# First batch's keys and values in one product, V loaded ahead of the queries, and another pattern of products of nothing

## The chip, the cores and the metric

The kernel runs on one core of one Trainium2 chip. The metric is the time of one execution on the device in microseconds. A core has TensorE for matrix products (in the profile PE, its weight loads PEld), VectorE (DVE), ScalarE (ACT) and GpSimd (POOL) for the rest, and SyncE (SP), which here issues nearly all DMAs. All engines run on their own, each in the order of its own list of instructions, and wait for each other by semaphores.

## The reference

Attention over 32 memory slots per head, then a mixture of experts. There are 8 batches, 8 heads, 576 tokens, head size 64; the experts have inner size 1024 and outer size 512.

```
a = softmax of phi over the 576 tokens
k_m = einsum('bhsm,bhsd->bhmd', a, k)
v_m = einsum('bhsm,bhsd->bhmd', a, v)
attn = softmax(q @ k_m^T / 8)
x = attn @ v_m, heads side by side: 4608 x 512
logits = x @ w_gate + modality_bias[modality_id]
e = argmax(logits); gate = its softmax probability
out = gate * (relu(x @ w1[e]) @ w2[e])
```

All arrays are float32.

## The kernel before

The kernel goes through the eight batches one after the other. For each batch it makes a memory of keys and values (`mem_max`, `mem_top`, `mem_exp`, `mem_sums`, then `kv_products` and `kv_divide`), turns them (`keys_turn`, `values_turn`), forms scores with the queries (`scores`, L420 in the profile), softens and normalises them on VectorE and ScalarE (`soften`, `normalise`) and splits the result into an upper and a lower part (`a_split`, tiles xah and xal, for the second half of the tokens xbh and xbl). The values are multiplied into the first expert weights (`value_products`, L561, tiles vwh and vwl), so that `hidden` (L594) gets from the attention weights straight to the inner layer, and `outputs` (L623) does the second expert product. Every one of these products is done as three terms of upper and lower parts. One expert is guessed at the start (`guess`), its weights are loaded, and a second pass for other experts runs only if the guess is wrong for some token; with these inputs it does not run.

The order of the work is written by a planner. There are two lists of stages, `attention` and `experts`; each stage has a kind (`TAKES` gives what it is thought to take on TensorE and what chain of other engines follows), the stages it comes after, a due place in the progress of the experts, and a `floor`, a planner's time before which it is not put in. `weave` merges the two lists by these numbers, and what it calls in turn is what each engine's list gets. The floors stand for the landing of loads. `plan_first` writes the stages of batch 0 up to its second scores, by hand.

At the start TensorE has nothing to do until the first loads land. `warm(n)` issues n products of a zero tile called `busy` into a PSUM bank that nobody reads (L152); `warm(BUSY)` does 38 of them at once, and `nothing(n)` stages stand between the stages of `plan_first`.

For batch 0 keys and values are separate in the kernel before. `kv_products(0, range(1))` multiplies the softened phi with the keys (L310 into the tile pair, 72 products), then with the column of ones for the sums (L319, 8 products). The values come in two pieces: five of nine chunks behind the keys, the other four behind the first scores (L310 into the tiles pe). `kv_divide` divides the keys (L340) and later the values (L338). From batch 1 on one call does both, with 128 columns instead of 64. A float32 product stands in the trace as two products and two weight loads, so that the 72 products of the keys are x144 there.

`load_kv`, `load_queries` and `load_phi` issue loads on SyncE's queue. For batch 0 the order is phi, K, the queries' first four chunks, V, the other five chunks; then come the token types, the gate's weights, and behind `guess` the two halves of the first expert weights (raw1), the second ones (raw2, in four loads), and batch 1's phi, K, V and queries (`more_keys`). The second expert weights are split in `first_w2` (casts on ScalarE L653, rests on GpSimd L654).

PSUM has two pairs of banks, pair0 and pair1 (`pair_of_banks`), and four single banks `pe`. The name "pa" is the first bank of pair0, "mem" the first of pair1.

## Time and profile before

| what | us |
|---|---|
| median of 3 runs (lowest, highest) | 410.91 (410.58, 411.28) |
| the profiled execution | 410.64 |
| its span in the trace | 408.9 |
| TensorE busy | 390.9 |
| VectorE busy | 238.7 |
| ScalarE busy | 143.7 |
| first product of L594 | 32.07 from the span's start |
| first product of L623 | 39.95 |

Times in the trace are from the span's start. A row of the timeline has the start, the time from the first to the last of merged instructions, engine, line, operation, what it writes and reads, shapes and count, and in brackets how long the engine was idle before and what ended that. "issue" there is time in which the engine waited for nothing that the profile shows. A busy TensorE is not TensorE at its peak, since products overlap in the pipeline. From 34 us to the end TensorE has hardly a gap.

### The profile page before, as it was taken

How to read it: one execution, taken by the hardware profiler on the slowest of the kernel's cores; microseconds unless marked ns; L12 is line 12 of the kernel's file. 1: busy time of each engine (PE TensorE's matmuls, PEld its weight loads, DVE VectorE, ACT ScalarE, POOL GpSimd, SP SyncE). 2: the span in 40 equal slices, each digit the busy share in tenths (PEclk: the TensorE clock that was granted, in tenths of full speed). 3: DMA queues.
4: the chain of work that ended last, by engine and by line, in shares of the span. 5: the costliest groups of instructions: out<-in, count | busy, mean ns of one | idle time of the engine just before them, and what ended most of it. 6: DMA issues, size and time to landing. Idle time of an engine off the chain costs nothing.

```text
span 408.9 us, 10298 instructions
## 1 busy us (share of the span) xinstructions
PE 390.9 (96%) x4350; PEld 312.4 (76%) x4350; DVE 238.7 (58%) x581; ACT 143.7 (35%) x342; POOL 39.6 (10%) x79
## 2 busy tenths in 40 slices
PE   8679998999999999999999999999999999989994
PEld 6437796688858879688867879687877879778983
DVE  3555773976688566773487447774388537861400
ACT  1218143433333325343442425242343424341410
POOL 3326302001100200002000200002000110000000
PEclk9758999999999999999999999999999999999998
DMA  7999046824471292526711274432602011341112
GB/s 233 358 387 340 30 111 209 304 101 139 144 282 31 81 332 69 211 73 207 252 27 27 83 264 140 151 133 63 222 2 51 27 29 28 129 157 26 28 27 58
DMA packets 28968, 56.92 MB, mean 139 GB/s; under 512 B 3312, under 2 KB 8432, under 8 KB 28912
## 3 DMA queue, kind: packets, MB, share of 16 engines
q1 hardware_dynamic: 28624, 56.16, 41.4%
q8 instruction: 36, 0.59, 0.6%
q14 instruction: 20, 0.16, 0.1%
q10 hardware_dynamic: 288, 0.01, 0.0%
HBM read 37.29 MB, written 18.87 MB: 137 GB/s over the span
## 4 chain that ended last, share of the span: by engine, by line
PE 87%; DVE 3%; ACT 3%; issue 3%; DMA 2%; POOL 1%; SPq 0%; ACTq 0%; POOLq 0%
PE pe L623 49%; PE pe L594 23%; PE pe L561 4%; PE pair L420 3%; PE pair L310 3%; DMA q_sb<-in_q_dram 2%; PE pair L508 1%; PE pair L140 1%; DVE hl L606 1%; ACT exp L283 1%; ACT hh L603 1%; ACT ob L636 1%; PE pair L561 0%; PE pair L152 0%; PE pair L274 0%
## 5 line engine op out<-in xcount | busy, mean ns | idle before, releaser
L623 PE MATMUL pe<-w2h,hh 128*128 128x512 f32 x288 | 117.9, 409 | 0.4 <-DVE hl L606 0.4
L623 PE MATMUL pe<-w2h,hl 128*128 128x512 f32 x288 | 112.5, 390 | 0.0
L623 PE MATMUL pe<-w2l,hh 128*128 128x512 f32 x288 | 110.4, 391 | 0.0
L606 DVE SCALAR_TENSOR_TENSOR hl<-pe,hh 128x256 fp32r<-128x256 f32 (+2 forms) x160 | 58.6, 393 | 53.8 <-ACT hh L603 53.2
L623 PEld LDWEIGHTS pe<-w2h,hh 128*128 128x128 f32 x288 | 54.0, 188 | 25.3 <-issue 12.9
L603 ACT ACTIVATE hh<-pe 128x256 fp32r<-128x256 f32 (+2 forms) x160 | 53.7, 362 | 38.9 <-PE pe L594 38.5
L623 PEld LDWEIGHTS pe<-w2l,hh 128*128 128x128 f32 x288 | 54.0, 188 | 12.0
L623 PEld LDWEIGHTS pe<-w2h,hl 128*128 128x128 f32 x288 | 54.2, 188 | 9.4
L636 ACT ACTIVATE ob<-pe,gates 128x512 f32<-128x512 f32 x36 | 24.7, 689 | 82.6 <-PE pe L623 41.9
L594 PE MATMUL pe<-xbh,vwh 128*128 128x320 f32 x128 | 39.8, 311 | 0.0
L594 PE MATMUL pe<-xbl,vwh 128*128 128x320 f32 x128 | 39.6, 309 | 0.0
L594 PE MATMUL pe<-xbh,vwl 128*128 128x320 f32 x128 | 39.5, 309 | 0.0
L594 PE MATMUL pe<-xah,vwh 128*128 128x256 f32 x128 | 37.1, 292 | 0.2 <-DVE hl L606 0.2
L594 PE MATMUL pe<-xal,vwh 128*128 128x256 f32 x128 | 36.2, 285 | 0.1
L594 PE MATMUL pe<-xah,vwl 128*128 128x256 f32 x128 | 35.3, 283 | 0.0
L249 POOL TENSOR_TENSOR t2sums<-exp 128x512 f32<-128x512 f32 x7 | 9.0, 1286 | 262.2 <-ACT exp L283 262.2
L594 PEld LDWEIGHTS pe<-xah,vwh 128*128 128x128 f32 x128 | 24.7, 193 | 3.0 <-ACT xah L488 1.7
L447 DVE STREAM_TRANSPOSE a<-pair 128x256 f32<-128x256 f32 (+1 forms) x32 | 13.6, 461 | 21.3 <-PE pair L420 21.3
L594 PEld LDWEIGHTS pe<-xal,vwh 128*128 128x128 f32 x128 | 24.6, 192 | 0.6 <-DVE xal L491 0.3
L594 PEld LDWEIGHTS pe<-xbh,vwh 128*128 128x128 f32 x128 | 24.1, 188 | 0.5 <-issue 0.2
L594 PEld LDWEIGHTS pe<-xbl,vwh 128*128 128x128 f32 x128 | 24.1, 188 | 0.3
L594 PEld LDWEIGHTS pe<-xah,vwl 128*128 128x128 f32 x128 | 24.0, 191 | 0.3 <-issue 0.3
(117 smaller groups left out, 444.1 us busy)
## 6 DMA issues: line engine op xcount, KB each, us to landing
kv_sb<-in_k_dram SPq DMA_DIRECT2D x8, 1152.0 KB, 6.4
kv_sb<-in_v_dram SPq DMA_DIRECT2D x8, 1152.0 KB, 8.8
out_dram<-ob SPq DMA_DIRECT2D x64, 128.0 KB, 2.4
q_sb<-in_q_dram SPq DMA_DIRECT2D x7, 1152.0 KB, 6.4
ph<-in_phi_dram SPq DMA_DIRECT2D x8, 576.0 KB, 4.3
raw<-in_moe_w_dram SPq DMA_DIRECT2D x2, 1024.0 KB, 9.5
raw<-in_moe_w_dram SPq DMA_DIRECT2D x1, 1280.0 KB, 12.4
out_dram<-ob SPq DMA_DIRECT2D x4, 256.0 KB, 2.1
```

Of the source, the lines that this page charges most:

```text
L140: nc.tensor.transpose(dst, src, ident[:rows, :rows])
L249: eng.tensor_tensor(t2, src[:, :, 0:4 * M], src[:, :, 4 * M:8 * M], op=op)
L283: nc.scalar.activation(px[:, :, cs], px[:, :, cs], AF.Exp)
L310: nc.tensor.matmul(kvp[g][M * j:M * (j + 1)], lhsT=pe[half, j, c * M:(c + 1) * M], rhs=kv_sb[half, ts.start:ts.stop, j, c * D:(c + 1) * D] ...
L420: nc.tensor.matmul(sc[g][M * j:M * (j + 1), a, c0 * BL:(c0 + n) * BL].rearrange("p (c t) -> p c t", t=BL), lhsT=kTs[b % 2][p0:p0 + BL, u, ...
L447: nc.vector.transpose(a[:, g].rearrange("p a c m -> p a (c m)"), sc[g][:, :, RA * part * BL:(RA * part + n) * BL])
L561: nc.tensor.matmul(pvs[g][M * j:M * (j + 1), :], lhsT=vT[b][rows, j, :], rhs=raw1[rows, j, cols], start=True, stop=True, tile_position=(D ...
L594: nc.tensor.matmul(ph[:, 0:n], lhsT=(vl if k == 2 else vh)[:, g, cols], rhs=xl if k == 1 else xh, start=(g == k == 0), stop=(g == NG - 1 a ...
L603: nc.scalar.activation(hs[0][:, f, h0:h0 + p1 - p0], ph[:, p0:p1], AF.Relu)
L606: nc.vector.scalar_tensor_tensor(hl, ph[:, p0:p1], 0.0, hh.bitcast(F32), op0=ALU.max, op1=ALU.subtract)
L623: nc.tensor.matmul(po, lhsT=tile_columns(hl if n == 1 else hh, f, t), rhs=(w2l if n == 2 else w2h)[:, f, :], start=(f == n == 0), stop=(f ...
L636: nc.scalar.activation(ob, po, AF.Copy, scale=gate_of(b, t))
```

## The change

The keys and values of batch 0 are multiplied together, as in the other batches, in one call of `kv_products(b)` into one pair of banks; `kv_divide(b)` divides both. V is loaded ahead of the queries. The first 38 products of nothing become 92 small ones (32 x 64 instead of 128 x 256) and two large ones (128 x 512, twice as wide as before). Between the stages of `plan_first` the products of nothing are all of the large kind, and there are fewer of them ahead of the keys (2 and 6 instead of 4 and 22) and some more behind. The turned keys and values of batch 0 go to pair0 instead of pair1, and some planner's floors are later.

```
-    BUSY = 38
+    BUSY = 92, 2
...
-    busy = const.tile([P, 256], BF16, name="busy")
+    busy = const.tile([P, 512], BF16, name="busy")
...
-    def warm(n):
+    def warm(n, small=False, name="pa"):
         if n > 0:
-            idle = bank("pa")
+            idle = bank(name)
             for _ in range(n):
-                nc.tensor.matmul(idle[:, 0:256], lhsT=busy[:, 0:P], rhs=busy, start=True, stop=True)
+                if small:
+                    nc.tensor.matmul(idle[0:BL, 0:64], lhsT=busy[:, 0:BL], rhs=busy[:, 0:64], start=True, stop=True)
+                else:
+                    nc.tensor.matmul(idle, lhsT=busy[:, 0:P], rhs=busy, start=True, stop=True)
...
-    def kv_products(b, ts, banks=None, cs=range(QC)):
+    def kv_products(b):
...
+        pk = pair_of_banks(1)
+        live["psum"] = pk[:, :, 2 * D]
+        live["kvp"] = pk[:, :, 0:2 * D].rearrange("p g (t d) -> p g t d", t=2)
+        for c in range(QC):
...
-                        kvp[g][M * j:M * (j + 1)], lhsT=pe[half, j, c * M:(c + 1) * M],
-                        rhs=kv_sb[half, ts.start:ts.stop, j, c * D:(c + 1) * D],
+                        live["kvp"][M * j:M * (j + 1), g], lhsT=pe[half, j, c * M:(c + 1) * M],
+                        rhs=kv_sb[half, :, j, c * D:(c + 1) * D],
...
-        live["pkv"] = pair_of_banks(1)
+        live["pkv"] = pair_of_banks(1 if b else 0)
...
-            live["pkv"] = pair_of_banks(1)
+            live["pkv"] = pair_of_banks(0)
...
+        nothing(2)
+        add(("exp", 0), "first exp", [("top", 0)], mem_exp, 0)
+        nothing(6)
+        add(("prepare",), "nothing", [], prepare)
+        add(("sums", 0), "first sums", [("exp", 0)], mem_sums, 0)
+        add(("kv", 0), "kv0", [("exp", 0)], kv_products, 0, floor=11.7)
+        turns(0, 0, 13.1)
+        add(("kn", 0), "kvn", [("kv", 0)], kv_divide, 0)
+        turns(0, 1, 13.1)
+        add(("more", 0), "nothing", [], more_keys, 0)
         nothing(4)
-        add(("exp", 0), "first exp", [("top", 0)], mem_exp, 0)
-        nothing(22)
-        add(("prepare",), "nothing", [], prepare)
-        turns(0, 0, 9.6)
-        add(("sums", 0), "first sums", [("exp", 0)], mem_sums, 0)
-        turns(0, 1, 9.6)
-        add(("k", 0), "k", [("exp", 0)], kv_products, 0, range(1), floor=8.5)
-        add(("kn", 0), "kn", [("k", 0), ("sums", 0)], kv_divide, 0, range(1))
-        v = range(1, 2)
-        add(("v", 0, 0), "v1", [], kv_products, 0, v, two_banks, range(RB), floor=12.8)
+        add(("kT", 0), "kT", [("kn", 0)], first_keys)
+        nothing(2)
         for k in range(2):
-            turns(1, k, 14.3)
-        add(("kT", 0), "kT", [("kn", 0)], first_keys)
-        nothing(6)
+            turns(1, k, 14.8)
         add(("s", 0, 0), "s0", [("kT", 0), ("qt", 0, 0, 1)], scores, 0, 0, RA)
         add(("e", 0, 0, 0), "e", [("s", 0, 0)], soften, 0, 0, None, 0)
-        add(("v", 0), "v2", [], kv_products, 0, v, None, range(RB, QC))
-        add(("vn", 0), "vn", [("v", 0)], kv_divide, 0, v)
+        nothing(3)
+        add(("kvT", 0), "vT", [("s", 0, 0)], first_values)
         add(("e", 0, 0, 1), "e", [], soften, 0, 0, None, 1)
         nothing(3)
-        add(("kvT", 0), "vT", [("vn", 0)], first_values)
-        add(("more", 0), "nothing", [], more_keys, 0)
         add(("n", 0, 0, 2), "n", [("e", 0, 0, 1)], normalise, 0, 0)
-        nothing(3)
-        add(("vw", 0, 0), "vwp", [("kvT", 0)], value_products, 0, 0, pair_(0), floor=17.0)
+        add(("vw", 0, 0), "vwp", [("kvT", 0)], value_products, 0, 0, pair_(0), floor=18.2)
         add(("vwu", 0, 0), "vwu", [("vw", 0, 0)], value_upper, 0)
-        add(("vw", 0, 1), "vwp", [], value_products, 0, 1, pair_(1), floor=19.7)
+        nothing(4, "pe")
+        add(("vw", 0, 1), "vwp", [], value_products, 0, 1, pair_(1), floor=21.0)
+        nothing(6, "pe")
...
-            stage(experts, ("w2", c), "w2", [], first_w2, c, floor=23.4 if c < W2N else 25.6)
+            stage(experts, ("w2", c), "w2", [], first_w2, c, floor=24.3 if c < W2N else 26.4)
...
-    plan_steps(0, evenly(1.9, 0.25))
+    plan_steps(0, evenly(1.4, 0.25))
...
-        load_kv(0, 0)
+        for t in range(2):
+            load_kv(0, t)
         load_queries(0, 0, RA)
-        load_kv(0, 1)
         load_queries(0, RA, RB)
...
-        warm(BUSY)
+        warm(BUSY[0], True)
+        warm(BUSY[1])
```

On TensorE the first place is the end of the opening products of nothing and the turn of phi's maxima (tile top) behind them. Before:

```order
L152 LDWEIGHTS busy
L152 MATMUL pair_154<-busy 128x256
L140 MATMUL pair_217<-ident,top 128x128 [waits DVE_49,Pool_49]
L152 LDWEIGHTS busy
L152 MATMUL pair_243<-busy 128x256 [waits PE_49]
```

and now:

```order
L154 LDWEIGHTS busy
L154 MATMUL pair_154<-busy 32x64
L156 LDWEIGHTS busy
L156 MATMUL pair_247<-busy 128x512 [waits PE_49]
L156 LDWEIGHTS busy
L156 MATMUL pair_247<-busy 128x512
L141 MATMUL pair_274<-ident,top 128x128 [waits DVE_49,Pool_49]
```

The turn of top (old L140, new L141) stood behind 76 instructions of nothing and now stands behind 188.

The second place on TensorE is the products of softened phi (tile exp) with keys and values (kv_sb), and the sums behind them. Before, the values (into pe) follow the keys' sums at once:

```order
L310 MATMUL pair_318<-kv_sb,exp 32x64 [waits DVE_49,DMAHW3_49,PE_49,Activation_49]
L310 MATMUL pair_318<-kv_sb,exp 32x64 x39
L310 MATMUL pair_318<-kv_sb,exp 32x64 [waits Activation_49]
L310 MATMUL pair_318<-kv_sb,exp 32x64 x31
L319 MATMUL pair_318<-ones_c,sums 32x1 [waits DVE_49,Pool_49]
L319 MATMUL pair_318<-ones_c,sums 32x1 x7
L310 MATMUL pe<-kv_sb,exp 32x64 [waits DMAHW5_49]
L310 MATMUL pe<-kv_sb,exp 32x64 x39
```

and now:

```order
L307 MATMUL pair_355<-kv_sb,exp 32x128 [waits DMAHW3_49,DVE_49,DMAHW4_49,PE_49,Activation_49]
L307 MATMUL pair_355<-kv_sb,exp 32x128 x39
L307 MATMUL pair_355<-kv_sb,exp 32x128 [waits Activation_49]
L307 MATMUL pair_355<-kv_sb,exp 32x128 x31
L315 MATMUL pair_355<-ones_c,sums 32x1 [waits DVE_49,Pool_49]
L315 MATMUL pair_355<-ones_c,sums 32x1 x7
L156 LDWEIGHTS busy
L156 MATMUL pair_451<-busy 128x512 [waits PE_49]
```

The first product now waits for two loads, K and V, where it waited for K alone; products of nothing stand where the values stood, and the values' 72 products of their own are gone.

SyncE's first loads stood in this order (ph is phi, q_sb the queries):

```order
L159 DMA ph_102<-in_phi_dram 128x4x288
L162 DMA kv_sb<-in_k_dram 128x4x576
L166 DMA q_sb_99<-in_q_dram 128x4x256
L162 DMA kv_sb<-in_v_dram 128x4x576
L166 DMA q_sb_99<-in_q_dram 128x4x320
```

and now stand in this one:

```order
L163 DMA ph_102<-in_phi_dram 128x4x288
L166 DMA kv_sb<-in_k_dram 128x4x576
L166 DMA kv_sb<-in_v_dram 128x4x576
L170 DMA q_sb_99<-in_q_dram 128x4x256
L170 DMA q_sb_99<-in_q_dram 128x4x320
```

V has moved ahead of the first part of the queries; nothing else on this queue has moved.

## The prediction

> **What bounds the kernel now.** The first page gives the frame: TensorE is busy 96% of the span, and its forty slices are thin only at the start, where the granted clock is low as well.

> ```profile
> span 408.9 us, 10298 instructions
> PE 390.9 (96%) x4350; PEld 312.4 (76%) x4350; DVE 238.7 (58%) x581; ACT 143.7 (35%) x342; POOL 39.6 (10%) x79
> PE   8679998999999999999999999999999999989994
> PEclk9758999999999999999999999999999999999998
> q8 instruction: 36, 0.59, 0.6%
> ```

> So the rest is one dense row of products, and what the change can win or lose is the moment when that row begins. The timeline of TensorE shows how it gets there (start, length, line; in brackets the idle time before).

> ```profile
> 8.18 0.30 PE L140 MATMUL pair<-ident,top 128*128 128x128 f32 x1 [0.41 <-DVE peak L183]
> 9.23 2.57 PE L152 MATMUL pair<-busy 128*128 128x256 bf16 x22
> 11.73 1.66 PE L310 MATMUL pair<-kv_sb,exp 64*32 64x64 f32 x144
> 13.54 0.24 PE L319 MATMUL pair<-ones_c,sums 64*32 64x1 f32 x8
> ...
> 17.66 0.23 PE L319 MATMUL pair<-ones_c,sums 64*32 64x1 f32 x5 [3.87 <-issue]
> 17.79 1.30 PE L310 MATMUL pe<-kv_sb,exp 64*32 64x64 f32 x75
> 21.21 0.74 PE L420 MATMUL pair<-q_sb,kT 32*32 32x128 f32 x31
> 23.89 0.80 PE L420 MATMUL pair<-q_sb,kT 32*32 32x128 f32 x33 [1.95 <-issue]
> 28.28 3.87 PE L561 MATMUL pair<-raw,vT 64*32 64x512 f32 x32
> 32.07 0.58 PE L594 MATMUL pe<-xah,vwh 128*128 128x256 f32 x1
> 39.95 0.40 PE L623 MATMUL pe<-w2h,hh 128*128 128x512 f32 x1
> ```

> Twice TensorE halts inside a group of equal products, for 3.87 and 1.95 us, with no engine named as releaser. Between the halts lie 127 products (the rest of L319, 80 of L310, two turns, six of nothing, 31 scores) and as many weight loads: 254 instructions. Queue q8 moves instructions in packets of 0.59 MB / 36 = 16 KB. One such packet starts in each of these windows, 15.00 to 15.02, 21.42 to 21.45 and 27.65 to 27.68:

> ```profile
> q8 instruction: 1, 0.02, 385.3%
> q8 instruction: 1, 0.02, 219.8%
> q8 instruction: 1, 0.02, 227.3%
> ```

> My reading: a block holds 256 instructions, entering one asks for the next, and the packet waits in DMA engines full of data. Entered at 17.66, packet at 21.43, running again at 23.89: **6.2 us from the request to the instructions**. As long as the DMA is full, TensorE gets no more than 256 instructions in 6.2 us.

> The second loss is the clock. Busy time of TensorE, and after the POOL column the granted clock, DMA share and GB/s:

> ```profile
> 12.75:16.16 3.41, 0.89 (x72) 0.67 (x55) 1.21 (x3) 0.00 (x0) 0.00 (x0) 1.00 1.14 306
> 16.16:33.23 17.07, 12.82 (x266) 6.47 (x266) 8.21 (x20) 5.00 (x14) 5.59 (x22) 0.50 1.05 387
> ```

> After a stretch in which TensorE worked 0.89 of 3.41 us the clock was 0.50 for 17 us, over exactly the work that leads to L594. [...]

> **The change part by part.** Durations are the profiled execution's: 410.64 us, 1.7 over its span and 0.27 under the median of 410.91.

> *Small products.* 38 of 256 columns become 92 of 64 columns and two of 512.

> ```profile
> 1.10 6.66 PE L152 MATMUL pair<-busy 128*128 128x256 bf16 x38 [1.10 <-POOL busy L951]
> ```

> One old product took 6.66 / 38 = 0.175 us. A quarter of the columns gives 0.044 below, the price of a whole one 0.175 above. L310, 144 products of 64 columns in 1.66 us, shows that issuing is no such price, so I take 0.044 to 0.055: 4 to 5 us. With a memset twice as wide (0.3 us) they end at 5.4 to 6.5 and the two large ones at about 7, before L140 needs TensorE at 8.18. They are hidden; from 0.065 us each they are not.

> *Where the blocks end.* Before, the first halt stood after 221 products, 442 instructions, so the block ahead ended at about 186. Now 94 products are 188: TensorE crosses there at 8.2, with L140, not at 12.0 inside the key products. At up to 6.2 us the next block is there by 14.4. The next end falls at 79% of the joint key and value products, the third in the first value product of L555 (old L561), the fourth in L588 (old L594) behind the second scores. 64 value products of the old v2 and dozens of small ones no longer stand between.

> *Keys and values together.* They need V, and V now loads ahead of the queries. Issue and time to landing (K, queries, V, the first weights in two halves, then the second weights):

> ```profile
> 2.32 1.43 SPq L162 DMA_DIRECT2D kv_sb<-in_v_dram  x1
> 12.28 1.68 SPq L194 DMA_DIRECT2D raw<-in_moe_w_dram  x1
> 14.15 1.54 SPq L197 DMA_DIRECT2D raw<-in_moe_w_dram  x1
> ...
> kv_sb<-in_k_dram SPq DMA_DIRECT2D x1, 1152.0 KB, 8.3
> q_sb<-in_q_dram SPq DMA_DIRECT2D x1, 512.0 KB, 9.2
> kv_sb<-in_v_dram SPq DMA_DIRECT2D x1, 1152.0 KB, 11.7
> raw<-in_moe_w_dram SPq DMA_DIRECT2D x1, 1024.0 KB, 8.7
> raw<-in_moe_w_dram SPq DMA_DIRECT2D x1, 1024.0 KB, 10.4
> raw<-in_moe_w_dram SPq DMA_DIRECT2D x1, 1280.0 KB, 12.4
> ```

> K landed at 9.5 (issued at 1.24), the queries at 11.0 (issued at 1.77), V at 14.0. Without the queries' 1.45 us ahead of it V lands at 12.6, the queries at 14.0. V lands between 12.6 (strictly in turn) and 14.0 (as before); I take 12.6, since the others landed in turn. The weights keep their place: 20.0, 22.7, 26.6. TensorE starts at 12.6, 0.9 later than before. The later batches already do this product:

> ```profile
> 63.45 2.25 PE L310 MATMUL pair<-kv_sb,exp 64*32 64x128 f32 x144
> 72.16 1.09 PE L561 MATMUL pe<-raw,vT 64*32 64x512 f32 x16
> ```

> 2.25 us for keys and values at the full clock: done at 14.9, where the next block has come (14.4), and the sums at 15.1.

> *From there to L588.* Reciprocals 0.4, keys 0.63, the values' two copies 0.5 now ahead of the turned keys' copy 0.37 on ScalarE, two large products of nothing that wait for it (0.47): scores from 17.6 to 18.3, their queries turned by 16.3. Before, the scores ended at 24.76 and this chain followed:

> ```profile
> 29.58 0.77 DVE L479 STREAM_TRANSPOSE aT<-a 128x256 f32<-128x256 f32 x2
> 31.29 0.63 ACT L488 CAST xah<-aT 128x512 fp32r<-128x512 f32 x1
> 31.96 0.69 DVE L491 TENSOR_TENSOR xal<-aT,xah 128x512 fp32r<-128x512 f32 x1 [1.60 <-ACT xah L488]
> ```

> That is 5.6 us to aT, 0.63 to xah, 0.69 to xal: 23.9, 24.6, 25.3. Beside it TensorE turns the values, waits for their copy (20.4), runs three large ones (0.7), the first value product from 21.0 (weights 20.0, block 14.4 + 6.2 = 20.6) for 1.0, four large ones (0.9), the second from 23.0 (weights 22.7) for 1.0, six large ones (1.4). L588 can start at 25.4; it stood at 32.07.

> *From L588 to the outputs.* Before: 7.88 us, the first 1.2 at half clock. At 0.117 us a product (2.57 / 22) 48 of them and 1.1 of scores are 6.7: outputs at 32.1. ScalarE could be late, since two casts of the second weights (landing 26.6, two in 1.15) stand ahead of its first relu at 27.8; TensorE needs that result near 29. Its eight casts and eight relus, 0.63 and 0.4 each, end at 34.8, needed at 35.3. These joints are tight; I add 0.3: 32.4 against 39.95, **7.55 us**.

> *Behind it.* The second half of batch 0 had 1.85 us to spare:

> ```profile
> 49.52 0.83 DVE L491 TENSOR_TENSOR xbl<-aT,xbh 128x640 fp32r<-128x640 f32 x1 [0.85 <-ACT xbh L488]
> 52.20 0.31 PE L594 MATMUL pe<-xbh,vwh 128*128 128x320 f32 x1
> ```

> VectorE's chain ran 9.1 us from the last hl (41.2); now from about 35.0 to 44.1, and TensorE comes at 32.4 + 12.25 = 44.65. That still fits. Batch 1 is far from its loads: its key products at 63.45 move to 56. So the gain is kept: 410.64 - 7.55 = 403.1, by the median 403.4.

> **The rivals.**

> *The clock falls for one stage.* Six large products (1.4 us) replace 22 (2.57), so TensorE rests from 10.7 to 12.6. A stretch worked 26% lost the clock, the one before it kept it; mine would be worked some 40%, or the rest falls across two. At half clock 75 products of L310 took 1.30, 1.5 times as long each; 1.5 to 2 times 2.25 costs 1.1 to 2.3 us, giving 405.1. [...]

> *The clock stays half until about 30,* as over the 17 us above, where 75% busy did not bring it back. Value products 3.87 instead of 2.2, large ones double, keys and values up to 4.5: L588 near 30.4, outputs near 37, gain 3 us: 407.9.

> *The halts are not fetches* but belong to the places (L319, the scores) under the full DMA, and return there with the clock loss. Then the old first value part (1.30 us) leaves the path, the start is 0.9 later, the halts stay: 410.5. [...]

> *The small products are dear.* One mechanism, at L154: above 0.065 us each they push L140 and all behind it. At 0.148 they have eaten the 7.6 us; at the upper end, 0.175, they end 10.1 us later than affordable: 413.4, slower.

> **How the numbers follow.** Forecast 0.50 (401.5 to 404.2, the tight joints either way and V up to 1 us late); clock lost once 0.28; half until 30 0.10; no fetches 0.07; dear small products 0.05. The range runs from 401.5 to 408.3, leaving out the last two and the edges. A measurement here tells 0.2% (0.8 us) from nothing. Faster: 0.50 + 0.28 + 0.10 + 0.02 of the fourth = 0.90; same 0.04; slower 0.06.

> **What would show it.** L154's 92 products in 4 to 5 us; L307 starting near 12.6, on V's landing; no idle by "issue" above 1 us before 30; L555 near 21, L588 near 25.4, the first L617 near 32.4; granted clock 1.00 from 6 us on. I am wrong if L141 starts after 8.5, if a halt of several us stands elsewhere, or if the shift at L617 isn't the shift at the end.

## The result, and the profile after

The changed kernel takes 404.04 us (median of 4 runs, 403.22 to 405.46) where the kernel before took 410.84 beside it: a ratio of 0.983, with a 95% interval of 0.981 to 0.986. Measured again twice, it took 404.77 and 403.74. Three executions of the kernels below took 635 to 1293 us, and every median and range leaves them out. The runs do not scatter around one value, they go with the clock. Of the 13 runs of this kernel five kept a mean granted clock of 0.997 or more and took 403.0 to 403.9; the other eight, at 0.989 to 0.995, took 403.95 to 406.0.

The profiled execution is one of the slower ones, 405.46 us. Its page (busy time and instructions of each engine, busy tenths in 40 slices, granted clock, and the instruction queue):

```profile
span 403.6 us, 10100 instructions
PE 387.7 (96%) x4251; PEld 309.4 (77%) x4254; DVE 238.8 (59%) x581; ACT 143.7 (36%) x342; POOL 39.9 (10%) x79
PE   5989998999999999999999999999999999989994
PEclk9799999999999999999999999999999999999998
q8 instruction: 35, 0.57, 0.6%
```

The share of TensorE is the same 96%; what is shorter is the thin part at the start. The timeline of TensorE there:

```profile
1.31 4.75 PE L154 MATMUL pair<-busy 128*32 128x64 bf16 x92 [1.31 <-POOL busy L944]
9.69 0.45 PE L141 MATMUL pair<-ident,top 128*128 128x128 f32 x1 [3.20 <-DVE peak L187]
14.22 2.98 PE L307 MATMUL pair<-kv_sb,exp 64*32 64x128 f32 x144
...
20.10 1.07 PE L414 MATMUL pair<-q_sb,kT 32*32 32x128 f32 x64
24.23 1.09 PE L555 MATMUL pair<-raw,vT 64*32 64x512 f32 x16
...
28.36 0.47 PE L588 MATMUL pe<-xah,vwh 128*128 128x256 f32 x1
35.58 0.40 PE L617 MATMUL pe<-w2h,hh 128*128 128x512 f32 x1
```

The 92 small products take 4.75 us. Keys and values are one group (L307), the first scores (L414) are a whole group, and neither halt of before is there. The first L617 stands at 35.58 instead of 39.95: 4.37 us earlier, not the 7.55 of the prediction. Two things at the start are later than forecast. The windows of the same execution show one, the landing times (the last column, from issue) the other:

```profile
5.52:8.93 3.41, 0.92 (x18) 0.61 (x16) 1.16 (x3) 0.00 (x0) 1.45 (x7) 1.00 1.05 398
8.93:15.76 6.83, 6.06 (x75) 2.93 (x79) 4.51 (x13) 1.25 (x2) 0.46 (x6) 0.50 1.05 349
15.76:35.00 19.24, 17.16 (x339) 10.73 (x326) 13.81 (x30) 9.81 (x25) 11.18 (x27) 1.00 1.04 369
```

```profile
kv_sb<-in_k_dram SPq DMA_DIRECT2D x1, 1152.0 KB, 9.5
kv_sb<-in_v_dram SPq DMA_DIRECT2D x1, 1152.0 KB, 12.0
```

After a stretch worked 0.92 of 3.41 us the clock is half for 6.8 us, up to 15.76 and so over the first half of L307; then it is back for all the rest of the work, where before it stayed half for 17. And V, issued at 1.78, lands 12.0 later, at 13.8 rather than at 12.6. In this execution K is late as well (9.5 from its issue at 1.24, where the kernel before has 8.3), and so is phi ahead of it (7.0 where the kernel before has 5.4): the loads were slow from the first one on.

### The profile page after: what moved, and what is told of

It is laid out like the page before. It is cut to its first block, busy times and chain, and to the rows that moved or that the text cites. A ratio compares the mean times of both kernels' runs of the same rounds, so it can differ in the third digit from the quotient of the medians.

```text
span 403.6 us, 10100 instructions
## 1 busy us (share of the span) xinstructions
PE 387.7 (96%) x4251; PEld 309.4 (77%) x4254; DVE 238.8 (59%) x581; ACT 143.7 (36%) x342; POOL 39.9 (10%) x79
## 4 chain that ended last, share of the span: by engine, by line
PE 90%; DVE 3%; ACT 2%; DMA 2%; issue 1%; POOL 1%; ACTq 0%; POOLq 0%
PE pe L617 50%; PE pe L588 23%; PE pair L307 4%; PE pe L555 4%; PE pair L414 3%; DMA ph<-in_phi_dram 2%; PE pair L502 1%; PE pair L156 1%; PE pair L141 1%; DVE hl L600 1%; ACT exp L287 1%; PE pair L278 1%; PE pe L156 1%; ACT hh L597 1%; PE pair L555 1%
## 5 line engine op out<-in xcount | busy, mean ns | idle before, releaser
L617 PE MATMUL pe<-w2h,hh 128*128 128x512 f32 x288 | 117.9, 409 | 0.4 <-DVE hl L600 0.4
L617 PE MATMUL pe<-w2h,hl 128*128 128x512 f32 x288 | 112.6, 391 | 0.0
L617 PE MATMUL pe<-w2l,hh 128*128 128x512 f32 x288 | 110.4, 391 | 0.0
L617 PEld LDWEIGHTS pe<-w2h,hh 128*128 128x128 f32 x288 | 54.0, 188 | 25.4 <-issue 12.9
L617 PEld LDWEIGHTS pe<-w2l,hh 128*128 128x128 f32 x288 | 54.0, 188 | 12.0
L617 PEld LDWEIGHTS pe<-w2h,hl 128*128 128x128 f32 x288 | 54.2, 188 | 9.3
L588 PE MATMUL pe<-xbh,vwh 128*128 128x320 f32 x128 | 39.8, 311 | 0.0
L588 PE MATMUL pe<-xbl,vwh 128*128 128x320 f32 x128 | 39.6, 309 | 0.0
L588 PE MATMUL pe<-xbh,vwl 128*128 128x320 f32 x128 | 39.5, 309 | 0.0
L588 PE MATMUL pe<-xah,vwh 128*128 128x256 f32 x128 | 36.9, 291 | 0.2 <-DVE hl L600 0.2
L588 PE MATMUL pe<-xal,vwh 128*128 128x256 f32 x128 | 35.9, 283 | 0.0
L588 PE MATMUL pe<-xah,vwl 128*128 128x256 f32 x128 | 35.3, 283 | 0.0
L588 PEld LDWEIGHTS pe<-xah,vwh 128*128 128x128 f32 x128 | 24.4, 191 | 1.4 <-DVE hl L600 0.7
L588 PEld LDWEIGHTS pe<-xal,vwh 128*128 128x128 f32 x128 | 24.5, 191 | 0.3
L588 PEld LDWEIGHTS pe<-xbh,vwh 128*128 128x128 f32 x128 | 24.1, 188 | 0.5 <-issue 0.2
L588 PEld LDWEIGHTS pe<-xbl,vwh 128*128 128x128 f32 x128 | 24.1, 188 | 0.3
L588 PEld LDWEIGHTS pe<-xah,vwl 128*128 128x128 f32 x128 | 24.0, 191 | 0.3 <-issue 0.3
L588 PEld LDWEIGHTS pe<-xbh,vwl 128*128 128x128 f32 x128 | 24.1, 188 | 0.0
## 6 DMA issues: line engine op xcount, KB each, us to landing
kv_sb<-in_k_dram SPq DMA_DIRECT2D x8, 1152.0 KB, 5.9
kv_sb<-in_v_dram SPq DMA_DIRECT2D x8, 1152.0 KB, 9.4
q_sb<-in_q_dram SPq DMA_DIRECT2D x7, 1152.0 KB, 7.3
raw<-in_moe_w_dram SPq DMA_DIRECT2D x2, 1024.0 KB, 8.6
raw<-in_moe_w_dram SPq DMA_DIRECT2D x1, 1280.0 KB, 11.0
```

What stands on the lines that cost most here:

```text
L588: nc.tensor.matmul(ph[:, 0:n], lhsT=(vl if k == 2 else vh)[:, g, cols], rhs=xl if k == 1 else xh, start=(g == k == 0), stop=(g == NG - 1 a ...
L617: nc.tensor.matmul(po, lhsT=tile_columns(hl if n == 1 else hh, f, t), rhs=(w2l if n == 2 else w2h)[:, f, :], start=(f == n == 0), stop=(f ...
```

## The experiments

Each was run beside the kernel before; the last three columns are from the profiled execution of each: when V landed, the time from the first to the last product of L307, and the first product of L617 (L628 in e1b).

| run | median (range), us | ratio, 95% interval | V landed | L307 | first L617 |
|---|---|---|---|---|---|
| c1_changed | 404.77 (403.89 to 406.03) | 0.984 (0.981 to 0.986) | 14.0 | 3.75 | 36.26 |
| c2_changed | 403.74 (403.02 to 404.23) | 0.981 (0.978 to 0.984) | 14.15 | 2.24 | 34.77 |
| e2_old_opening | 410.79 (407.16 to 412.23) | 0.997 (0.995 to 1.000) | 12.5 | 2.24 | 37.13 |
| e1_opening_alone | 421.97 (420.44 to 422.8) | 1.026 (1.024 to 1.029) | – | – | – |
| e1b_opening_alone | 421.51 (420.62 to 423.97) | 1.026 (1.020 to 1.031) | 14.9 | 1.92 (keys) | 43.85 |
| e3_v_behind | 407.51 (405.79 to 408.19) | 0.990 (0.988 to 0.993) | 15.5 | 4.09 | 38.33 |
| e4_84_10 | 403.85 (403.31 to 404.75) | 0.982 (0.980 to 0.984) | 12.6 | 2.90 | 34.15 |
| e4b_84_10 | 404.0 (403.86 to 404.05) | 0.983 (0.980 to 0.985) | 12.5 | 3.14 | 34.20 |
| e5_88_10 | 405.51 (404.02 to 406.2) | 0.986 (0.983 to 0.989) | 13.9 | 3.70 | 35.94 |
| e9_filled_rest | 406.78 (405.03 to 407.18) | 0.988 (0.984 to 0.992) | 12.4 | 3.30 | 36.76 |
| e8_short_path | 403.45 (403.2 to 404.71) | 0.982 (0.980 to 0.984) | 12.6 | 3.02 | 33.64 |
| e8b_short_path | 403.88 (403.31 to 404.98) | 0.983 (0.980 to 0.986) | 12.5 | 2.86 | 33.54 |

**The changed kernel as it is, twice.**

> The changed kernel as it is, as the yardstick for the other runs beside it: 403.2 to 405.5, median 404.0. If the clock theory holds, the runs that never lose the clock (granted clock 0.997 to 1.00) are near 403.3 and those that lose it once (about 0.99) 404.5 to 405.5; if the spread has another cause, time and granted clock do not go together.

> The changed kernel again, as the measure for the others of this call: 404.0 to 405.4; with V landing near 14.0 and the clock lost once 405, with the clock kept 403.6.

The first of the two, then the second, from the timeline of TensorE:

```profile
14.13 3.75 PE L307 MATMUL pair<-kv_sb,exp 64*32 64x128 f32 x144 [3.39 <-DMA kv_sb<-in_v_dram]
```

```profile
8.36 0.30 PE L141 MATMUL pair<-ident,top 128*128 128x128 f32 x1 [1.80 <-DVE peak L187]
...
14.29 2.22 PE L307 MATMUL pair<-kv_sb,exp 64*32 64x128 f32 x143 [1.87 <-DMA kv_sb<-in_v_dram]
19.43 1.07 PE L414 MATMUL pair<-q_sb,kT 32*32 32x128 f32 x64
23.41 1.09 PE L555 MATMUL pair<-raw,vT 64*32 64x512 f32 x16
27.55 0.47 PE L588 MATMUL pe<-xah,vwh 128*128 128x256 f32 x1
34.77 0.40 PE L617 MATMUL pe<-w2h,hh 128*128 128x512 f32 x1
```

In both V lands near 14 and L307 starts on it. In the first the clock was half from 13.98 to 17.39, over L307; it was lost in the rest that waits for V (0.18 of 3.41 us worked). In the second it was half from 9.09 to 12.50, over products of nothing, where it cost the path nothing; it was lost in another rest, the one between the opening's products and L141 (1.80 us idle). The 1.5 us between 3.75 and 2.24 are the 1.5 us between the two first L617 (36.26 and 34.77): in these two profiles the place where the clock is lost makes the difference.

**The old opening put back into the changed kernel** (112 instructions fewer on TensorE, so that every block end falls 112 instructions later in the work). In the trace of the kernel before, 254 products and weight loads and two semaphore instructions lie between the two halts: 256 in all, the block of the prediction.

```
-    BUSY = 92, 2
+    BUSY = 38
...
-        warm(BUSY[0], True)
-        warm(BUSY[1])
+        warm(BUSY, True)
```

with `warm(n, True)` issuing the old 128 x 256 product.

> The changed kernel with the opening of before: 38 products of 256 columns in place of 92 small and two large ones, so 112 instructions fewer ahead of everything. If TensorE halts at block ends (fetch theory), the ends move by 112 instructions: the first lies at 30% of the joint key and value products (crossed at 13.3 to 14.5), so that the second, in the first scores, cannot be passed before 19.5 to 20.7: a halt of 0.5 to 2 us appears in L413 at its first products, and the time is 0.5 to 2 us over the changed kernel at the same clock. If the halts belong to places (the sums, the scores) or to the DMA load, nothing of the kind moves: no halt, as in the changed kernel, and 403.3 to 404.0, since the longer opening also keeps the clock.

The timeline, at the first scores and in the key and value products and sums of batches 1 and 2:

```profile
17.82 0.29 PE L414 MATMUL pair<-q_sb,kT 32*32 32x128 f32 x1
19.47 1.38 PE L414 MATMUL pair<-q_sb,kT 32*32 32x128 f32 x63 [1.35 <-issue]
...
64.19 0.34 PE L307 MATMUL pair<-kv_sb,exp 64*32 64x128 f32 x8 [1.51 <-issue]
...
107.46 0.23 PE L315 MATMUL pair<-ones_c,sums 64*32 64x1 f32 x4 [1.16 <-issue]
```

The halt came where the count puts a block end, in the scores (called L413 in the expectation), and with nothing but the opening put back; the packet moved at 17.04. It also lost the clock from 19.65 to 26.48. The size was missed: 6.0 us over c1, which ran beside it. The expectation looked at batch 0 alone, but the ends behind it had moved too, into two groups that halt for 1.5 and 1.2 us. These halts and the 0.9 us at the first L617 cover the 3.3 us between the two profiled executions (409.32 against 406.03); the rest of the 6.0 us between the medians stands in no profile.

**The new opening put into the kernel before** (112 instructions more ahead of the same work).

```
-    BUSY = 38
+    BUSY = 92, 2
...
-        warm(BUSY)
+        warm(BUSY[0], "small")
+        warm(BUSY[1], "large")
```

> The kernel before with the opening of the change alone (92 small and two large products for its 38; the joint product, the loads and the other products of nothing stay as before): 112 instructions more ahead of everything. Fetch theory: the halts leave the sums and the scores and stand at the new block ends, in the key products at two thirds (short, up to 1.6 us), in the first part of the value products at four fifths (about 4 us) and in their second part; the clock is lost as before, and the time is 409 to 411. Place theory: the halts stay at the sums (L324) and in the first scores (L425), and the time is 410.5 to 411.3. If the opening alone were what brings the gain, it would be 404 to 406.

It became 11.3 us slower, far from every expectation. Its second run has the profile that shows where.

> The kernel before with the opening alone changed, a second time, to see where its 11.7 us go. Theory of instruction fetches: the block ends now fall inside the first key products, inside both parts of the separate value products and inside the second scores; every one costs about 6.2 us from the end before it, so halts by issue of 1 to 4 us stand in L315 (keys), in L315 into pe twice, with the clock lost as before; first L628 near 50 to 52 instead of 39.95, time 420 to 424. Rival (the clock): no more halts than the two of before, but the clock is half until 40 or later: L628 also near 50. Rival (that chip alone): the time is 409 to 412.

The timeline of TensorE, at the separate value products of batch 0 and at the sums (here L324) of batches 3 and 6:

```profile
15.18 0.84 PE L315 MATMUL pe<-kv_sb,exp 64*32 64x64 f32 x61
21.39 0.47 PE L315 MATMUL pe<-kv_sb,exp 64*32 64x64 f32 x16 [5.36 <-issue]
...
25.30 0.76 PE L315 MATMUL pe<-kv_sb,exp 64*32 64x64 f32 x39
29.92 0.65 PE L315 MATMUL pe<-kv_sb,exp 64*32 64x64 f32 x25 [3.86 <-issue]
...
147.47 0.25 PE L324 MATMUL pair<-ones_c,sums 64*32 64x1 f32 x11 [1.69 <-issue]
...
294.04 0.25 PE L324 MATMUL pair<-ones_c,sums 64*32 64x1 f32 x10 [1.28 <-issue]
```

The theory of fetches is right in kind: both parts of the value products halt, for 5.36 and 3.86 us; the keys' products, where a halt was expected too, have none. The places follow from the count. With an end at 186 instructions, as the prediction has it, and one every 256 behind it, the ends fall behind 64 of the 80 products of the first part and 40 of the 64 of the second; the halts stand behind 64 and 39. The expected place of the loss was half wrong. The first L628 is at 43.85, only 3.9 later than before, not at 50 to 52; the other 7.6 us go in batches 3 to 6 (which lose 8.2, while batch 2 wins 0.8). Each of these four halts among its 16 sums, after 5, 9, 7 and 6 of them, for 1.2 to 1.7 us. From batch 3 on a batch has 505 to 511 products, where four blocks are 512: it is nearly a whole number of blocks long, and an end that fell badly in batch 3 fell badly in the next three too. From the start of the key and value products of one batch to the next this kernel loses 3.5, 1.9, 1.4 and 1.5 us against the kernel before (in batch 3 the halt also took the clock for a window, 148.5 to 152.0). The opening's 92 small products are thus no gain by themselves: they are worth 6.0 us in one kernel and cost 11 in the other, by where the ends fall. Nor does the rest of the change gain by itself: with the old opening (e2) it can't be told from the kernel before (ratio 0.997, with an interval of 0.995 to 1.000). What the joint products, the other banks and the later floors are worth by themselves is not shown; the place of V was tried alone, as follows.

**V behind the queries' first part again.**

```
-        for t in range(2):
-            load_kv(0, t)
+        load_kv(0, 0)
         load_queries(0, 0, RA)
+        load_kv(0, 1)
```

> The changed kernel with V loaded behind the first part of the queries again. If the joint product starts on V's landing, it starts 1.0 to 1.45 us later (V about 15.2 where the changed kernel has 13.8) and the time rises by 0.7 to 1.4 us: 404.7 to 405.4. If the order of the loads does not matter, because the scores wait for the queries or the products of nothing stand in front anyway, it stays within 0.3 us of the changed kernel.

```profile
15.60 4.09 PE L307 MATMUL pair<-kv_sb,exp 64*32 64x128 f32 x144 [4.83 <-DMA kv_sb<-in_v_dram]
```

V lands 1.5 us later than in c1 (15.5 against 14.0), about the 1.45 us by which the queries' 512 KB landed behind K before. The time is 2.7 us over c1, more than expected; between the two profiled executions it is 2.2. With 4.8 us of rest the clock was half for two windows, 14.1 to 20.9, rather than for one, and L307 took 4.09 instead of 3.75. Loading V first is thus worth 1.5 us by its own landing; that the clock makes up all the rest is likely but not shown.

**What delays V.** Eight of the small products become large ones, with the same number of instructions, so that the opening runs nearly until L141; then, beside that kernel, four small products (8 instructions) more.

```
-    BUSY = 92, 2
+    BUSY = 84, 10
```

> The changed kernel with 84 small and 10 large products at the opening: the same 188 instructions, but TensorE works until about 8 us instead of 6.5. If the spread of the changed kernel is the clock that falls once in the rest before phi's maxima, the granted clock stays 1.00 from 6 us on in every run, the joint product takes 2.3 us instead of 3.0 and all runs lie at 402.8 to 403.6. If the clock is not the cause, the median stays at 404.0 with the same spread.

> The kernel with 84 small and 10 large products once more, as the yardstick for the two variants of it beside it: 403.3 to 404.8, median 403.9, the first instruction packet at about 12.5 us and V landing at 12.6.

```
-    BUSY = 92, 2
+    BUSY = 88, 10
```

> 88 small and 10 large products: eight instructions more, so that the first block end falls inside the opening and is crossed at about 6 to 8 us instead of at phi's maxima (8.7). Theory that a packet of instructions holds up the load that shares its DMA engine: the packet comes ahead of V's last bytes, V lands at 13.9 to 14.1 and not at 12.6, the joint product starts 1.3 to 1.4 us later and the time is 0.8 to 1.4 us over that of 84 and 10 (about 404.9). Rival, that a packet does not touch the loads: V at 12.6, the 0.33 us halt in the joint product is gone since its instructions come earlier, and the time is 0.2 to 0.4 us lower (403.6).

Time from issue to landing of K and V (issued at 1.24 and 1.78), in e4b first, then in e5, then of V in c2 (K took 8.2 there):

```profile
kv_sb<-in_k_dram SPq DMA_DIRECT2D x1, 1152.0 KB, 8.2
kv_sb<-in_v_dram SPq DMA_DIRECT2D x1, 1152.0 KB, 10.7
```

```profile
kv_sb<-in_k_dram SPq DMA_DIRECT2D x1, 1152.0 KB, 9.7
kv_sb<-in_v_dram SPq DMA_DIRECT2D x1, 1152.0 KB, 12.1
```

```profile
kv_sb<-in_v_dram SPq DMA_DIRECT2D x1, 1152.0 KB, 12.4
```

The first instruction packet, in the windows 12.52 to 12.55 of e4b, 8.82 to 8.85 of e5 and 11.95 to 11.98 of c2:

```profile
q8 instruction: 1, 0.02, 239.4%
q8 instruction: 1, 0.02, 225.8%
q8 instruction: 1, 0.02, 231.9%
```

It started at 12.54 in e4b, when V had landed, and nothing was late. In e5 the end is crossed in the opening, the packet started at 8.83, and K is 1.5 us late, V behind it 1.4. In c2 it started at 11.96, after K's landing and before V's, and V alone is late by 1.6. So in these profiles a load in whose time a packet of 16 KB falls lands 1.4 to 1.6 us later, and in e5 eight instructions were all that moved the packet. What V wins in e4b is given back in part, since the packet then comes too late for the joint products, which halt 80% through:

```profile
12.64 1.90 PE L307 MATMUL pair<-kv_sb,exp 64*32 64x128 f32 x115 [1.83 <-DMA kv_sb<-in_v_dram]
15.12 0.55 PE L307 MATMUL pair<-kv_sb,exp 64*32 64x128 f32 x23 [0.57 <-issue]
```

So the clock was kept in e4 and e4b as expected, but L307 took 2.90 and 3.14 us instead of 2.3, and the runs lie at 403.3 to 404.8 instead of 402.8 to 403.6. In e5 V came as late as the theory of the packet has it, and the median is 1.5 us over that of e4b.

**The rest filled.** To tell the price of the clock from that of V, eight more large products ahead of the joint ones (`nothing(6)` becomes `nothing(14)` behind the first exp).

> Eight more large products of nothing stand ahead of the key and value products (14 where 6 were), the opening is that of the changed kernel, so the first block end still falls at L141 and its packet near 11.8. Theory of two separate prices (the packet delays V by 1.4 us; the rest of TensorE from 9.7 to 14 loses the clock): V still lands near 14.0, but TensorE works until about 12.6, the clock stays 1.0, and L307 takes 2.2 to 2.3 us instead of 3.75; first L617 near 34.8 to 35.3 instead of 36.3, time 403.7 to 404.5. Rival (the rest that is left, 12.6 to 14.0, is enough to lose the clock): L307 again 3.0 to 3.75, L617 near 36.3, time 404.8 or more. Rival (a late V has nothing to do with the packet): V lands at 12.6 and the time is near 403.3.

```profile
15.04 0.74 PE L307 MATMUL pair<-kv_sb,exp 64*32 64x128 f32 x35 [0.70 <-issue]
...
22.04 0.38 PE L156 MATMUL pair<-busy 128*128 128x512 bf16 x1 [1.31 <-issue]
...
24.65 1.86 PE L555 MATMUL pair<-raw,vT 64*32 64x512 f32 x16
```

None of the three came. The clock was kept until 22.86 and V landed at 12.4, but the time is 3.0 us over c2, which ran beside it. Sixteen instructions more moved the third end from the first value product (L555) to the products of nothing behind the scores, so that it came sooner after the one before it: it halts there, the window that holds the halt is worked 1.48 of 3.42 us, and the clock is half over L555 (1.86 instead of 1.09). So here eight products that do nothing had a price by their sixteen instructions. Why the packet came at 12.50 here and at 11.96 in c2, with L141 at 8.30 and 8.36, stays open. V's price and the clock's were therefore not told apart by this run. For the clock c1 against c2 does it, 1.5 us. For V e5 against e4b does not, since e5 lost the clock over L307 too (13.63 to 17.05, L307 took 3.70). In c2 and e4b L307 had the full clock: V landed 1.6 us later in c2, and the first L617 is only 0.57 later, since e4b's early V runs into the halt.

**A shorter chain to the scores.** e4 with the sums' reciprocals ahead of the queries' turns on VectorE and the two products of nothing ahead of the scores moved.

```
-    BUSY = 92, 2
+    BUSY = 84, 10
...
-        turns(0, 0, 13.1)
         add(("kn", 0), "kvn", [("kv", 0)], kv_divide, 0)
+        turns(0, 0, 13.1)
...
-        nothing(4)
+        nothing(5)
...
-        nothing(2)
...
-        nothing(3)
+        nothing(4)
```

> The 84 and 10 kernel with the reciprocals of batch 0 ahead of the queries' transposes on VectorE, and with the two large products of nothing between the turned keys and the scores taken out of there (one goes ahead of the turn, one behind the scores; the count of instructions ahead of the value products stays). If the chain from the sums over reciprocals, keys and scores to xah and xal ends last, the scores start 1.0 to 1.2 us earlier (17.7) and the time falls by 0.7 to 1.2 us, to about 402.9. If the loads of the weights or the casts of the second weights end last, it stays within 0.2 us of the yardstick.

> The best version so far, beside the changed kernel on one chip: 403.2 to 403.9, that is 0.8 to 1.3 us under the changed kernel in the same call; first L617 near 33.6. If the gain over the changed kernel was a difference of the chips: within 0.4 us of it.

In the profiles of e8 and e8b the scores start at 18.0 and 17.8 and the first L617 is at 33.6 and 33.5, 1.1 to 1.2 earlier than in c2, and the clock was kept in each. Yet beside the changed kernel its median is 403.88 against 403.74. The expected 0.8 to 1.3 us aren't there; its gain over the changed kernel is smaller than the runs can tell, and so is e4's. No version measurably beats the changed kernel.

## Why the prediction was right, and where its steps were off

**The bound.** Right: the gain is in the start of the dense row. Both halts of before are gone, and e2 and e1b bring halts back by the opening alone, at places that follow from the count of its instructions. That the halts belong to the places (the third rival) is out: L414 halts in e2 and not in c1.

**Small products.** 4 to 5 us forecast; 4.75, 5.09 and 4.82 measured in the first profile, c1 and c2. In c1 and c2 L141 stands at 8.2 and 8.4 as forecast; in the first profile it is at 9.69, since phi landed late there. That is one of the prediction's own signs of being wrong (L141 after 8.5), though not by the small products.

**V at 12.6.** This term failed. The reason given, that the others landed in turn, holds in e4b (12.5). In the changed kernel V landed at 14.0 and 14.15 in c1 and c2, behind the packet, and at 13.8 in the first profile, where the packet came later (13.35) but phi and K were late too. The prediction had itself moved the first packet to the time before V's landing, and did not ask what else that packet would hold up. What made phi late in one execution stays open.

**The clock is kept (0.50) against lost once (0.28).** Both came, but the rival more often: it was lost in the start in all three profiles, and 8 of 13 runs lie below 0.997. That the rest ahead of L307 would leave the clock alone was the author's estimate: the last three windows at the full clock before were worked 88%, 100% and 26% (3.00, 3.41 and 0.89 of 3.41 us), and only the last lost it. The forecast looked for the danger in that rest. In c1 it lay there; in the first profile and in c2 it lay in the rest behind the small products, 3.20 and 1.80 us of idle time ahead of L141, which the prediction counted as hidden and did not weigh for the clock. The price was forecast at 1.1 to 2.3 us; L307 took 2.98 and 3.75 instead of 2.25, 0.7 and 1.5 us, and in c2 the loss cost nothing. The forecast time, 403.4, lies inside the range of the five runs that kept it.

**From the start of L307 to L617.** Forecast from 12.6 to 32.4, 19.8 us; in c2, with the full clock there, from 14.29 to 34.77, 20.5. To the scores it is 5.14 against the forecast 5.0, from there to L555 3.98 against 3.4, to L588 4.14 against 4.4, and to L617 7.22 against 7.0. The 0.6 us in the second stretch is the only one of size; in it TensorE stands 0.51 us until VectorE has read the scores (a, L441) and 0.35 us until the turned values are copied (vT, L372). The next block, forecast at 14.4, came at 15.1 in e4b, where it halts TensorE for 0.57 us; behind a late V that can't be seen.

**"So the gain is kept."** The prediction let everything behind L617 move by the same amount. It did not ask where the block ends fall in later batches. The first value product of batch 2, before (with the last of its weight loads, PEld) and then in c2:

```profile
113.34 1.73 PE L561 MATMUL pe<-raw,vT 64*32 64x512 f32 x16
114.02 0.14 PEld L561 LDWEIGHTS pe<-raw,vT 64*32 64x32 f32 x4 [0.51 <-issue]
```

```profile
108.03 1.09 PE L555 MATMUL pe<-raw,vT 64*32 64x512 f32 x16
```

Before, an instruction packet moved at 111.79, the last four of the 16 weight loads came after 0.51 us of idle time by issue, and the group took 1.73 us instead of 1.09. Up to batch 2 c2 is 5.2 us ahead of before (39.95 against 34.77 at the first outputs, 105.63 against 100.43 at batch 2's key and value products), from batch 3 on 5.96 (140.19 against 134.23, 402.97 against 397.01 at the last product). So 0.8 us of the gain, 0.6 of it in this group, came from a place that the prediction had not looked at. Another 0.5 us lie behind the last product, from which the span's end is 5.9 us away before and 5.4 in c2; no run shows why. The forecast of 7.55 us at the first L617 was 2.4 us too much in c2, 3.2 in the first profile and 3.9 in c1, and that the shift there is not the shift at the end is another of the prediction's own signs of being wrong. At the end c2's profiled execution misses the forecast by 1.1 us (404.23 against 403.1): the time was right partly by luck, because gains that nobody had forecast made up for half of what V and the longer chain took.

## What to carry over

In these kernels TensorE's instructions come in blocks of 256 (counted between the two halts before), and an edit that adds or removes some moves every end behind it, to the end of the program: 112 more in the opening of e1b put halts of 1.2 to 1.7 us into batches 3 to 6. Count the instructions up to each end, in later iterations too when an iteration is close to a whole number of blocks, and look at what is in flight when the packet comes and how soon the next end follows. An edit that looks like filling or like saving ("92 products of nothing") has to be measured in the kernel in which it stands: here the same opening won 6 us in one and lost 11 in the other.

## What the runs showed of the hardware that was not expected

**An instruction packet delayed the loads.** In the five profiles in which a packet started well before a load had landed, that load of 1152 KB was late: K by 1.5 us in e5 and V by 1.6 in c2 and 1.5 in c1 (against e4b), V by 1.4 in e3 and 0.9 in e1b (against the kernel before, with the same order of loads). The packet of 16 KB itself took 1.1 us on one of 16 DMA engines (in c2 231.9% of the 16 engines' 0.03 us). In the seven in which the first packet started no more than 0.1 us ahead of V's landing or later, V stood within 0.1 us of its place. A load was late without a packet, though: in the first profile, which is in neither group, phi was 1.5 us late, and no packet had started by then.

**From the packet to the work was nearly a constant.** TensorE ran again 2.3 to 2.8 us after its packet started, in all 17 halts of 0.3 us or more in these profiles. Some of them: 15.00 to 17.66 and 21.43 to 23.89 before, 17.04 to 19.47 and 61.90 to 64.19 in e2, 12.54 to 15.12 in e4b, 12.50 to 15.04 and 19.23 to 22.04 in e9, 18.83 to 21.39 and 27.51 to 29.92 in e1b. From one halt's end to that of the next, one block on, it was not: 6.2 us before, 7.0 in e9 and 8.5 in e1b, so the prediction's 6.2 us is the figure of one place.

**The clock went and came back at different shares of work.** Between two changes of the granted clock lay whole numbers of 3.41 us (17.07 at half before, 6.83 in the first profile). Windows of that length in a row, here of e2 and then of c2 (length, then busy time of TensorE; the granted clock is the third number from the end):

```profile
16.24:19.65 3.41, 1.51 (x29) 0.68 (x38) 1.57 (x2) 0.76 (x3) 2.79 (x14) 1.00 1.04 381
19.65:23.06 3.41, 2.62 (x66) 1.22 (x49) 2.08 (x5) 0.42 (x1) 2.86 (x9) 0.50 1.05 386
23.06:26.48 3.42, 3.01 (x20) 0.48 (x18) 3.07 (x8) 0.58 (x2) 0.15 (x1) 0.50 1.05 384
26.48:29.89 3.41, 3.41 (x34) 1.00 (x27) 1.27 (x3) 2.51 (x5) 0.00 (x0) 1.00 1.07 390
```

```profile
5.67:9.09 3.42, 1.56 (x20) 0.83 (x18) 2.40 (x8) 0.00 (x0) 1.31 (x8) 1.00 1.06 409
9.09:12.50 3.41, 3.33 (x11) 0.98 (x10) 2.15 (x4) 1.25 (x2) 0.00 (x0) 0.50 1.06 383
12.50:15.91 3.41, 1.62 (x118) 1.65 (x126) 1.49 (x5) 0.00 (x0) 0.00 (x0) 1.00 1.07 301
```
